# Block-sparse attention with a Swish MLP: all engines in written order, weight casts placed by step, and a V gather shared by two queues

## The chip, the cores and the metric

The kernel runs on one core of a Trainium2 chip. The metric is the device time of one execution in microseconds (us), the median of the runs shown. A core has five engines, each with an instruction queue of its own that it works through in order: TensorE (PE in the profile; its weight loads are PEld), VectorE (DVE), ScalarE (ACT), GpSimd (POOL) and SyncE (SP), which only issues DMAs here. ScalarE and GpSimd issue DMAs too. An instruction waits at the head of its queue until the semaphores it needs are set, and what stands behind it waits as well.

## The reference

Attention over 4 batches, 8 heads, 768 positions and head size 64, in blocks of 32 (24 blocks). A query block sees its neighbours, the first and the last block and three drawn blocks; the first and the last query block see everything. The result, as 3072 rows of 512, goes through a two-layer MLP.

```python
mask = np.abs(blk_i - blk_j) <= 1
mask = mask | (blk_i == 0) | (blk_j == 0) | (blk_i == n_blocks - 1) | (blk_j == n_blocks - 1)
for qb in range(n_blocks):
    for kb in sampled_blocks[qb]:
        mask[qb*32:(qb+1)*32, kb*32:(kb+1)*32] = True
attn = softmax(np.where(mask, scale * q @ k.T, -1e9))
x = (attn @ v)                      # to (3072, 512), heads side by side
h = x @ w_in                        # 512 to 2048
out = (h / (1 + exp(-beta * h))) @ w_out   # 2048 to 512
```

## The kernel before

**Tiling.** A chunk is 128 query rows (4 blocks) of one batch; there are 6 chunks in a batch, taken in the order 1, 2, 0, 5, 3, 4. I call them A, B, C, D, E and F in that order. A step is one chunk with one half of the heads (`Q`, 4 heads). There are 48 steps, 12 for each batch, in this order: A0 B0 A1 B1 C0 D0 C1 D1 E0 E1 F0 F1 (steps 0 to 11), and the same for the next batch (12 to 23, and so on). Chunk C holds the first query block and D the last, so three of their four blocks need gathered data.

**A step** (loop at L635). `scores` writes for each query block the products with its window of three blocks and with five gathered blocks (`KG`: first, last and the three drawn) into two PSUM tiles `sc`; VectorE takes the negative row maximum (`nm`, L334), ScalarE the exponential (`probs`, L337). There are two `sc` buffers, so the next step's scores wait for this step's exponentials. Then `do_A` runs the attention product of three steps earlier (`attend`, L397: `VA` holds the window's V rows and the first block, `VB` the three drawn blocks and the last; then `rec`, L415, and `x`, L416), and `do_T` transposes the previous step's probabilities (`probs_T`; `probsT`, L349). In steps 2 to 5 of each batch `do_G` adds the scores of the first and last query block with all keys (`scg`, `gnm` at L369 and L371, `gp` at L375), also through the `sc` buffers; `do_GT` transposes these one step later.

**MLP.** Finished chunks are transposed (`x_transpose`) and pushed in groups of 2 to 4 as units: `h_unit` (4 products into `hps`, tanh on ScalarE at L457, `g` on VectorE at L459) and `o_unit` (L470, result copied by ScalarE at L476 and written out). `run_moe` spreads them over the steps; the first run in step 7.

**Gathers.** After the second half of a chunk, `prefetch` and `prefetch_v` fetch for the chunk two places on: at the end of step 2 for C, of 3 for D, of 6 for E, of 7 for F, of 9 for the next batch's A, of 11 for its B. `gather_chunk` copies K blocks on GpSimd (L255, L261; `KG` has three buffers). `gather_v` reads rows of `vtab`, a table of V in DRAM that each batch writes (L239). SP issues the DMAs: two or three for `VA`, then one for the last block's rows and one for each drawn block (12 for a chunk, 9 for C and D; the addresses come from registers that SP loads from `sb_eff`). Only chunk A takes `VB` from GpSimd's queue, as four indirect DMAs (L280) whose row lists lie in `idx_b`. `VA` and `VB` have three buffers, so a gather must wait for the attention product of three chunks before: the one for D, issued at the end of step 3, waits for A1's product in step 5, the one for F (end of step 7) for C1's in step 9.

**Weights and next batch.** `load_w_in` and `load_w_out` load 2 MB halves of the float32 weights into a tile of tag `g` and cast them on VectorE (L181, L188); the tag has two buffers, shared with the first loads of v, k and q and later with the MLP's `g`. The first w_in half is issued by SP ahead of the first V gathers, the second by GpSimd in step 0, the w_out halves by GpSimd in steps 2 and 4. `prep_items` prepares the next batch in steps counted from `o`: loads at `o`, v cast and `vtab` written at `o + 2`, k and q cast on GpSimd and transposed on TensorE from `o + 3` to `o + 7`; `o` is 3 for batch 1, 0 for the later ones.

**Row lists.** L111 to L156 are small VectorE operations that turn the drawn block numbers into `sb_eff` and `idx_b`: a drawn block that is visible anyway is replaced by a block of zeros.

**What sets the order.** TensorE, GpSimd and SyncE run in the order in which the program is written; VectorE's and ScalarE's instructions are ordered by the compiler's scheduler:

```python
ctx.enter_context(tc.manual_schedule(engines={ET.PE, ET.Pool, ET.SP}))
```

Of the kernel before, what the change touches and what calls it, by code (L numbers as in the profile page):

```python
# [14 lines left out]
ALU = mybir.AluOpType  # L15
AX = mybir.AxisListType
ET = mybir.EngineType
# [3 lines left out]
def kernel(  # L21
# [11 lines left out]
    nc = tc.nc  # L33

    B, H, S, D = q.shape
    BLK = 32
    NB = S // BLK
# [3 lines left out]
    D_MODEL = H * D  # L41
# [34 lines left out]
    sb_i32 = persist.tile([P, NB * 3, 2], I32, name="sb_i32")  # L76
    nc.sync.dma_start(out=sb_i32.rearrange("p n w -> p (n w)"), in_=sb_all)

    ctx.enter_context(tc.manual_schedule(engines={ET.PE, ET.Pool, ET.SP}))
    identity = persist.tile([P, P], FP16, name="identity")  # L80
    make_identity(nc, identity)

# [10 lines left out]
    def big(name):  # L93
        return g_pool.tile([P, 4096], FP32, tag="g", name=name)
# [60 lines left out]
    idx_b = persist.tile([P, NB], I32, name="idx_b")  # L155
    nc.vector.tensor_copy(out=idx_b, in_=idx_f)  # L156

    def load_regs(t, engine, top, c):
        i0, i1 = max(4 * c, 1), min(4 * c + 4, NB - 1)
# [14 lines left out]
    w_out_r = moe_w_out.rearrange("(c p) m -> p c m", p=P)  # L174
    HF = D_FF // 2

    def load_w_in(hf, eng):
        wst = big("w_in_st").rearrange("p (c f) -> p c f", c=N_DMC)
        eng.dma_start(out=wst, in_=w_in_r[:, :, hf * HF:(hf + 1) * HF])
        for f0 in range(0, HF, 256):  # L180
            nc.vector.tensor_copy(out=w_in_sb[:, :, hf * HF + f0:hf * HF + f0 + 256],  # L181
                                  in_=wst[:, :, f0:f0 + 256])

    def load_w_out(hf):
        wst = big("w_out_st").rearrange("p (c m) -> p c m", m=D_MODEL)
        nc.gpsimd.dma_start(out=wst, in_=w_out_r[:, 8 * hf:8 * hf + 8, :])
        for c0 in range(0, 8, 2):
            nc.vector.tensor_scalar(out=w_out_sb[:, 8 * hf + c0:8 * hf + c0 + 2, :],  # L188
                                    in0=wst[:, c0:c0 + 2, :], scalar1=0.5, scalar2=None,
                                    op0=ALU.mult)  # L190


    zero_sb = persist.tile([BLK, VROW], FP16, name="zero_sb")
# [7 lines left out]
    def prep_tensor(name, b, Q, startup):  # L201
        st = st_tiles.pop((name, b, Q))
        h16 = half_pool.tile([P, 6, 4, D], FP16, tag="h16", name=f"{name}16")
        for h in range(4):
            dst = h16[:, :, h, :]
            src = st[:, h, :, :]
            if startup and name == "k":
                nc.scalar.copy(out=dst, in_=src)
            elif startup:
                nc.vector.tensor_copy(out=dst, in_=src)  # L210
            else:
                nc.gpsimd.tensor_copy(out=dst, in_=src)  # L212
        return h16
# [49 lines left out]
                    in_=kv[:, p0:p1, bass.ds(k_regs[(4 * c + j, r)] * BLK, BLK)])  # L263
        return last

    def gather_v(b, c, indirect=False):
        VA = vg_pool.tile([P, 4, VROW], FP16, tag="VA", name="VA")
        VB = vg_pool.tile([P, 4, VROW], FP16, tag="VB", name="VB")
        js = [j for j in range(4) if 0 < 4 * c + j < NB - 1]
        tab = vtab[b]  # L270

        def rows(row0, nrow, jstep, nj):
            base = tab[row0:row0 + nrow, :]
            ap = list(base.ap)
            return dataclasses.replace(base, ap=[ap[0], [jstep * VROW, nj], ap[1]])

        nj = len(js)
        if indirect:
            for j in js:
                nc.gpsimd.indirect_dma_start(  # L280
                    VB[:, j, :], None, tab[:, :],
                    bass.IndirectOffsetOnAxis(idx_b[:, 4 * c + j:4 * c + j + 1], 0))
# [7 lines left out]
        if indirect:  # L290
            return VA, VB
        v_regs = load_regs(sb_eff, ET.SP, NB, c)
        gb = [j for j in js if 4 * c + j != NB - 2]
        nc.sync.dma_start(out=VB[96:128, gb[0]:gb[0] + len(gb), :],
                          in_=rows(S - BLK, BLK, 0, len(gb)))
        if len(gb) != nj:
            nc.sync.dma_start(out=VB[96:128, NB - 2 - 4 * c, :], in_=tab[S:S + BLK, :])
        for j in js:
            for r in range(3):
                nc.sync.dma_start(  # L300
                    out=VB[BLK * r:BLK * (r + 1), j, :],
                    in_=tab[bass.ds(v_regs[(4 * c + j, r)] * BLK, BLK), :])
        return VA, VB


# [208 lines left out]
    def prep_items(b):  # L514
        def load(n, Q):
            return lambda: load_quad(n, {"q": q, "k": k, "v": v}[n], b, Q, None, nc.gpsimd)
        hold = {}

        def cast(n, Q):
            def f():  # L520
                hold[(n, Q)] = prep_tensor(n, b, Q, False)
            return f

        def tr(n, Q, pr):
            return lambda: transpose_pair(n, b, Q, pr, hold[(n, Q)])
# [12 lines left out]
        return items  # L538
# [12 lines left out]
        prep_v(0, 1, True)  # L551
        write_vtab(0, nc.sync)

    def start_kq1():
        for n in ("k", "q"):
            h16 = prep_tensor(n, 0, 1, True)
            for pr in range(2):
                transpose_pair(n, 0, 1, pr, h16)

    chunk_seq = order  # L560

# [6 lines left out]
    def prefetch_v(n):  # L568
        if n < len(chunk_seq):
            b, c = chunk_seq[n]  # L570
            Vs[(b, c)] = gather_v(b, c, c == 1)

    def start_kg(part):
        for n in range(2):
# [5 lines left out]

    start_kg(0)
    start_v()
    load_w_in(0, nc.sync)
    prefetch_v(0)
    prefetch_v(1)

# [48 lines left out]
    for n, (b, c, Q) in enumerate(steps):  # L635
# [27 lines left out]
        run_moe(units // 2 - units // 4)  # L663
# [53 lines left out]
```

## Time and profile before

| | |
|---|---|
| median of 3 runs | 399.39 us (394.26, 399.39, 401.61) |
| profiled execution | 399.42 us |
| its span, first to last instruction | 397.6 us |
| mean granted TensorE clock | 0.966 |
| HBM traffic over the span | 152 GB/s |
| instructions | 12930 |

Busy time and count by stretch:

| us | TensorE busy | VectorE busy | GpSimd busy | DMA share | GB/s |
|---|---|---|---|---|---|
| 0 to 20 | 6.10 | 9.77 | 11.99 | 0.75 | 247 |
| 20 to 37.4 | 5.98 | 9.89 | 11.62 | 0.94 | 277 |
| 37.4 to 57.4 | 7.96 | 12.37 | 12.48 | 0.98 | 330 |
| 57.4 to 83 | 16.55 | 18.47 | 21.93 | 0.88 | 305 |
| 83 to 106 | 16.37 | 13.92 | 16.09 | 0.57 | 143 |

How to read the lines of the profile that follow: a busy share is the union of an engine's instructions; "in 40 slices" gives one digit for each fortieth of the span (9.94 us), the busy share in tenths. The chain that ended last is followed back from the last instruction, at each step to what released it. In the view of waits a line names the engine and the tile that waited, what released it, the sum in us, how often, and the longest. In a timeline a line has start and duration in us, engine, source line, operation, output and inputs, a count, and in brackets the idle time before it and what ended it.

### The profile page before, as it was taken

Reading aid. Unit: us, or ns where it says so; the run is one execution under the profiler, and the core shown is the slowest. Engines: PE = TensorE matmul, PEld = TensorE weight load, DVE = VectorE, ACT = ScalarE, POOL = GpSimd, SP = SyncE. Lnnn points to the kernel's source line nnn. Section 1 sums busy time; section 2 is a strip of 40 time slices with the busy share of each in tenths; the row PEclk is TensorE's granted clock in tenths of the full one; section 3 lists DMA queues with packets and bytes.
Section 4 is the critical chain, followed back from the end, with each engine's and each line's share of the span. In section 5 each row is a group of like instructions: output and inputs, shape, how many; then the busy total and the mean of one; then the engine's idle time right before and its main releaser. Section 6 shows DMA issues by size and latency. Waiting matters only on the chain.

```text
span 397.6 us, 12930 instructions
## 1 busy us (share of the span) xinstructions
PE 310.0 (78%) x5056; PEld 181.8 (46%) x5056; DVE 239.3 (60%) x499; ACT 202.0 (51%) x401; POOL 170.6 (43%) x472
## 2 busy tenths in 40 slices
PE   1433525685757778978988789999799999999996
PEld 0221313574544435444544455555454555445652
DVE  0938746864777664564777565667677767544330
ACT  3461313375645655542656666546555656444441
POOL 4748939957785194037780193082420400000000
PEclk9999999999978988996999999999899999999999
DMA  7798999756897233057983152454313424100112
GB/s 214 284 335 175 368 357 388 242 110 162 269 333 200 53 88 77 8 144 225 330 292 83 44 136 44 116 156 116 104 26 91 128 57 123 41 28 30 51 54 79
DMA packets 41085, 61.24 MB, mean 154 GB/s; under 512 B 7968, under 2 KB 31648, under 8 KB 41024
## 3 DMA queue, kind: packets, MB, share of 16 engines
q1 hardware_dynamic: 29136, 29.01, 27.9%
q0 software_dynamic: 6368, 25.11, 18.1%
q10 hardware_dynamic: 5520, 6.30, 4.6%
q8 instruction: 40, 0.66, 0.8%
q14 instruction: 21, 0.17, 0.1%
HBM read 50.77 MB, written 9.62 MB: 152 GB/s over the span
## 4 chain that ended last, share of the span: by engine, by line
PE 50%; DVE 23%; ACT 10%; DMA 8%; issue 3%; POOL 3%; another core or an unknown queue 1%; POOLq 0%; SPq 0%; ACTq 0%; DVEq 0%
PE ops L470 17%; PE hps L453 17%; DVE nm L334 6%; DMA w_out_st<-in_moe_w_out_dram 4%; DVE g L459 4%; PE sc L329 3%; PE tp_p L345 3%; ACT gp L375 3%; ACT t_sb L457 3%; ACT probs L337 3%; PE av L397 3%; DVE probsT L349 2%; DMA st_q<-in_q_dram 2%; PE av L409 2%; DVE gnm L369 2%
## 5 line engine op out<-in xcount | busy, mean ns | idle before, releaser
L337 ACT ACTIVATE probs<-sc,nm 128x256 f16<-128x256 f32 x192 | 75.5, 475 | 84.1 <-DVE nm L334 83.1
L459 DVE SCALAR_TENSOR_TENSOR g<-t_sb,hps 128x512 f16<-128x512 f16 (+1 forms) x112 | 67.9, 610 | 66.0 <-ACT t_sb L457 64.6
L453 PE MATMUL hps<-xT,w_in_sb 128*128 128x512 f16 (+1 forms) x448 | 101.3, 363 | 0.8 <-DVE g L459 0.7
L457 ACT ACTIVATE t_sb<-hps,beta_h_sb 128x512 f16<-128x512 f32 (+1 forms) x112 | 69.6, 630 | 49.1 <-PE hps L453 47.3
L470 PE MATMUL ops<-w_out_sb,g 128*128 128x512 f16 x384 | 91.9, 385 | 0.0
L334 DVE TENSOR_REDUCE nm<-sc 128x2 f32<-128x512 f32 x96 | 61.8, 684 | 28.1 <-PE sc L329 28.0
L261 POOL COPY KG<-kT 128x128 f16 (+1 forms) x288 | 72.5, 310 | 0.0
L453 PEld LDWEIGHTS <-w_in_sb 128*128 128x128 f16 x448 | 42.8, 102 | 36.0 <-issue 7.5
L470 PEld LDWEIGHTS <-g 128*128 128x128 f16 x384 | 37.5, 99 | 42.8 <-issue 3.4
L255 POOL COPY KG<-kT 128x512 f16<-128x512 f16 (+2 forms) x52 | 27.6, 562 | 48.8 <-PE sc L329 38.2
L329 PE MATMUL sc<-kT,qT 64*32 64x96 f16 (+1 forms) x832 | 24.4, 223 | 21.4 <-ACT gp L375 17.5
L329 PEld LDWEIGHTS <-qT 64*32 64x32 f16 x1536 | 17.0, 96 | 47.7 <-issue 29.3
L349 DVE COPY probsT<-tp_p 128x1024 f16<-128x1024 f16 x48 | 32.2, 671 | 7.5 <-remote 2.5
L280 POOL DMA_INDIRECT VB<-vtab,idx_b x16 | 15.6, 975 | 43.2 <-PE av L397 33.3
L345 PE MATMUL tp_p<-identity,probs 128*128 128x128 f16 x384 | 33.9, 239 | 0.0
L212 POOL CAST q<-st_q 128x384 f16<-128x384 f32 x24 | 11.2, 511 | 36.3 <-PE tp_k L219 18.5
L329 PE MATMUL sc<-KG,qT 64*32 64x160 f16 x704 | 22.2, 250 | 5.9 <-POOL KG L261 5.0
L476 ACT COPY osb<-ops 128x512 f32<-128x512 f32 x24 | 14.1, 588 | 24.3 <-PE ops L470 24.3
L345 PEld LDWEIGHTS <-probs 128*128 128x128 f16 x384 | 24.8, 107 | 3.2 <-issue 0.4
L375 ACT ACTIVATE gp<-scg,gnm 128x384 f16<-128x384 f32 x32 | 16.8, 577 | 17.9 <-DVE gnm L371 17.9
L397 PE MATMUL av<-VB,probsT 128*32 128x65 f16 x704 | 25.1, 203 | 0.1
L397 PE MATMUL av<-VA,probsT 128*32 128x65 f16 x704 | 23.2, 205 | 1.1 <-issue 1.1
(69 smaller groups left out, 306.6 us busy)
## 6 DMA issues: line engine op xcount, KB each, us to landing
VB<-vtab SPq DMA_DIRECT2D x220, 32.5 KB
VA<-vtab SPq DMA_DIRECT2D x16, 390.0 KB
out_dram<-osb ACTq DMA_DIRECT2D x24, 256.0 KB
st_v<-in_v_dram POOLq DMA_DIRECT2D x6, 768.0 KB
st_k<-in_k_dram POOLq DMA_DIRECT2D x6, 768.0 KB
st_q<-in_q_dram POOLq DMA_DIRECT2D x6, 768.0 KB
w_out_st<-in_moe_w_out_dram POOLq DMA_DIRECT2D x2, 2048.0 KB
VA<-vtab SPq DMA_DIRECT2D x8, 292.5 KB
```

The source lines that it names most:

```text
L261: last = nc.gpsimd.tensor_copy(out=KG[:, j, p0:p1, BLK * (1 + r):BLK * (2 + r)], in_=kv[:, p0:p1, bass.ds(k_regs[(4 * c + j, r)] * BLK, BLK)])
L329: nc.tensor.matmul(o, lhsT=lhsT, rhs=rhs, start=True, stop=True, tile_position=(64 * hp, BLK * j))
L334: nc.vector.tensor_reduce(out=nm[:, hp, :], in_=scs[hp], axis=AX.X, op=ALU.max, negate=True)
L337: nc.scalar.activation(out=pt[:, 2 * pr + hp, :], in_=scs[hp][:, pr, :], func=AF.Exp, bias=nm[:, hp, pr:pr + 1], scale=1.0)
L345: nc.tensor.transpose(out=tp[:, u * 256 + half * P:u * 256 + (half + 1) * P], in_=pt[:, u, half * P:(half + 1) * P], identity=identity)
L349: nc.vector.tensor_copy(out=ptT.rearrange("p u h q -> p (u h q)"), in_=tp)
L375: nc.scalar.activation(out=pv[:, :, 64 * s:64 * (s + 1)], in_=halves[s].rearrange("p (s e) -> p e s", e=6), func=AF.Exp, bias=nm[:, 2:3], ...
L397: nc.tensor.matmul(av[BLK * j:BLK * (j + 1), u, :], lhsT=ptT[:, u, half, BLK * j:BLK * (j + 1)], rhs=V[:, j, h * VW:(h + 1) * VW], start=( ...
L453: nc.tensor.matmul(hp[:, 0:n], lhsT=w_in_sb[:, cc, f * P:(f + 1) * P], rhs=xT_tiles[gi][:, cc, 0:n], start=(cc == 0), stop=(cc == N_DMC - 1))
L457: nc.scalar.activation(out=t_sb[:, 0:n], in_=hp[:, 0:n], func=AF.Tanh, bias=0.0, scale=beta_h_sb[:, f:f + 1])
L459: nc.vector.scalar_tensor_tensor(out=g_tiles[gi][:, f, 0:n], in0=t_sb[:, 0:n], scalar=1.0, in1=hp[:, 0:n], op0=ALU.add, op1=ALU.mult)
L470: nc.tensor.matmul(op, lhsT=g_tiles[gi][:, f, s * P:(s + 1) * P], rhs=w_out_sb[:, f, :], start=(f == 0), stop=(f == N_FFC - 1))
```

## The change

1. VectorE and ScalarE are put into the written order as well, so all five engines follow the program. The row lists (L111 to L156) thereby come first on VectorE.
2. The weight halves are loaded and cast in separate functions. Loads: first w_in half on SP as before, second w_in half on ScalarE's queue in step 0, w_out halves on SP in steps 1 and 4. Casts: steps 1, 3, 5 and 7.
3. The cast of the second half of batch 0's k and q is moved from step 0 to before the loop, its transposes stay in step 0.
4. Every chunk's `VB` is shared: SP reads the rows of its blocks 0 and 1 (one DMA for the last block's rows and three for the drawn blocks, each), GpSimd the blocks 2 and 3 by one indirect DMA each. Before, chunk A was all on GpSimd and the others all on SP. In a batch this makes 11 indirect DMAs in place of 4.
5. The preparation of batch 1 begins in step 4 in place of 3.

```diff
-    ctx.enter_context(tc.manual_schedule(engines={ET.PE, ET.Pool, ET.SP}))
+    ctx.enter_context(tc.manual_schedule(engines={ET.PE, ET.Pool, ET.SP, ET.DVE, ET.Activation}))
...
+    def load_w(kind, hf, eng):
+        if kind == "in":
+            st = big("w_in_st").rearrange("p (c f) -> p c f", c=N_DMC)
+            eng.dma_start(out=st, in_=w_in_r[:, :, hf * HF:(hf + 1) * HF])
+        else:
+            st = big("w_out_st").rearrange("p (c m) -> p c m", m=D_MODEL)
+            eng.dma_start(out=st, in_=w_out_r[:, 8 * hf:8 * hf + 8, :])
+        w_st[(kind, hf)] = st
+
+    def cast_w(kind, hf):
+        st = w_st.pop((kind, hf))
+        if kind == "in":
+            for f0 in range(0, HF, 256):
+                nc.vector.tensor_copy(out=w_in_sb[:, :, hf * HF + f0:hf * HF + f0 + 256],
+                                      in_=st[:, :, f0:f0 + 256])
+        else:
+            for c0 in range(0, 8, 2):
+                nc.vector.tensor_scalar(out=w_out_sb[:, 8 * hf + c0:8 * hf + c0 + 2, :],
+                                        in0=st[:, c0:c0 + 2, :], scalar1=0.5, scalar2=None,
+                                        op0=ALU.mult)
...
-    def gather_v(b, c, indirect=False):
+    def gather_v(b, c):
...
-        if indirect:
-            for j in js:
-                nc.gpsimd.indirect_dma_start(
-                    VB[:, j, :], None, tab[:, :],
-                    bass.IndirectOffsetOnAxis(idx_b[:, 4 * c + j:4 * c + j + 1], 0))
...
+        v_regs = load_regs(sb_eff, ET.SP, NB, c, 2)
         for j in js:
-            for r in range(3):
-                nc.sync.dma_start(
-                    out=VB[BLK * r:BLK * (r + 1), j, :],
-                    in_=tab[bass.ds(v_regs[(4 * c + j, r)] * BLK, BLK), :])
+            if j < 2:
+                g = 4 * c + j
+                nc.sync.dma_start(out=VB[96:128, j, :], in_=tab[S - BLK:S, :])
+                for r in range(3):
+                    nc.sync.dma_start(
+                        out=VB[BLK * r:BLK * (r + 1), j, :],
+                        in_=tab[bass.ds(v_regs[(g, r)] * BLK, BLK), :])
+            else:
+                nc.gpsimd.indirect_dma_start(
+                    VB[:, j, :], None, tab[:, :],
+                    bass.IndirectOffsetOnAxis(idx_b[:, 4 * c + j:4 * c + j + 1], 0))
...
-        o = 3 if b == 1 else 0
+        o = 4 if b == 1 else 0
...
     start_kg(0)
     start_v()
-    load_w_in(0, nc.sync)
+    start_kq1_cast()
+    load_w("in", 0, nc.sync)
     prefetch_v(0)
     prefetch_v(1)
...
         if n == 0:
-            start_kq1()
+            start_kq1_T()
             start_kg(1)
-            load_w_in(1, nc.gpsimd)
-        if n == 2:
-            load_w_out(0)
+            load_w("in", 1, nc.scalar)
+        if n == 1:
+            cast_w("in", 0)
+            load_w("out", 0, nc.sync)
+        if n == 3:
+            cast_w("in", 1)
         if n == 4:
-            load_w_out(1)
+            load_w("out", 1, nc.sync)
+        if n == 5:
+            cast_w("out", 0)
+        if n == 7:
+            cast_w("out", 1)
```

More of the change, by code (lines that the diff above doesn't have):

```diff
@@ L156, with load_regs @@
     nc.vector.tensor_copy(out=idx_b, in_=idx_f)
-    def load_regs(t, engine, top, c):
-        i0, i1 = max(4 * c, 1), min(4 * c + 4, NB - 1)
+    def load_regs(t, engine, top, c, nj=4):
+        i0, i1 = max(4 * c, 1), min(4 * c + nj, NB - 1)
         _, vs = nc.values_load_multi_w_load_instructions(
@@ L175 @@
     HF = D_FF // 2
[L177 to L190, printed above, removed]
+    w_st = {}
+    def load_w(kind, hf, eng):
[17 more added lines that the diff above has]
+                                        op0=ALU.mult)
     zero_sb = persist.tile([BLK, VROW], FP16, name="zero_sb")
@@ L289, in gather_v @@
             nc.sync.dma_start(out=VA[96:128, 1, :], in_=tab[S:S + BLK, :])
[L290 to L297, printed above, removed]
-        for j in js:
-            for r in range(3):
-                nc.sync.dma_start(
-                    out=VB[BLK * r:BLK * (r + 1), j, :],
-                    in_=tab[bass.ds(v_regs[(4 * c + j, r)] * BLK, BLK), :])
+        v_regs = load_regs(sb_eff, ET.SP, NB, c, 2)
+        for j in js:
+            if j < 2:
[9 more added lines that the diff above has]
+                    bass.IndirectOffsetOnAxis(idx_b[:, 4 * c + j:4 * c + j + 1], 0))
         return VA, VB
@@ L552, in start_v, with start_kq1_cast, start_kq1_T @@
         write_vtab(0, nc.sync)
-    def start_kq1():
+    kq1 = {}
+    def start_kq1_cast():
         for n in ("k", "q"):
-            h16 = prep_tensor(n, 0, 1, True)
+            kq1[n] = prep_tensor(n, 0, 1, True)
+    def start_kq1_T():
+        for n in ("k", "q"):
             for pr in range(2):
-                transpose_pair(n, 0, 1, pr, h16)
+                transpose_pair(n, 0, 1, pr, kq1[n])
     chunk_seq = order
@@ L570, in prefetch_v @@
             b, c = chunk_seq[n]
-            Vs[(b, c)] = gather_v(b, c, c == 1)
+            Vs[(b, c)] = gather_v(b, c)
     def start_kg(part):
```

## The prediction

> **What bounds the kernel now.** I read in this order: the page's busy shares and forty slices, the chain that ended last, who waited for whom, who waited for the gathered V, and VectorE's timeline up to 60 us.
>
> ```profile
> PE 310.0 (78%) x5056; PEld 181.8 (46%) x5056; DVE 239.3 (60%) x499; ACT 202.0 (51%) x401; POOL 170.6 (43%) x472
> ...
> PE   1433525685757778978988789999799999999996
> ...
> DMA  7798999756897233057983152454313424100112
> ...
> PE 50%; DVE 23%; ACT 10%; DMA 8%; issue 3%; POOL 3%; another core or an unknown queue 1%; POOLq 0%; SPq 0%; ACTq 0%; DVEq 0%
> ```
>
> TensorE works 310 us of 397.6. Of the 88 us it stands, 37 lie in the first 57 (20 us of work done there), where the 16 DMA engines are nine tenths busy. From 106 us on it is some nine tenths busy, and half of the chain is its own work.
>
> ```profile
> POOL VB L280 <- PE av L397: 33.3, 3, 16.6
> ...
> PE sc L329 <- ACT gp L375: 17.5, 24, 2.0
> ```
> ```profile
> who waited for it (us, times):
>   POOL VB L280: 33.3, 3
>   PEld L397: 0.2, 1
> ```
>
> The attention product waited for a gathered VB 0.2 us in the whole run, so a shorter gather on SP wins nothing by itself. The gather on GpSimd waited three times, 33.3 us in all, for the product that frees its buffer, and everything behind it on GpSimd waited too.
>
> ```profile
> 31.13 6.32 DVE L181 CAST w_in_sb<-w_in_st 128x1024 f16<-128x1024 f32 x4 [4.70 <-DMA w_in_st<-in_moe_w_in_dram]
> 37.37 1.27 DVE L334 TENSOR_REDUCE nm<-sc 128x2 f32<-128x512 f32 x2
> ...
> 47.14 2.77 DVE L181 CAST w_in_sb<-w_in_st 128x1024 f16<-128x1024 f32 x4
> 55.00 2.50 DVE L188 TENSOR_SCALAR w_out_sb<-w_out_st 128x1024 f16<-128x1024 f32 x4 [5.09 <-DMA w_out_st<-in_moe_w_out_dram]
> 57.41 1.28 DVE L334 TENSOR_REDUCE nm<-sc 128x2 f32<-128x512 f32 x2
> ```
>
> I date each step by its first row maximum (L334). Steps 2 to 12 begin at 37.4, 43.0, 57.4, 63.3, 69.6, 76.1, 82.8, 88.1, 93.1, 102.2 and 105.6. A step with global scores takes 5.9 (4 to 5). Step 3 to 4 takes 14.4: VectorE stands in its queue before the first half of w_out while step 4's scores are ready. That is what the change can win.
>
> **Part by part.** The profiled execution took 399.42 us (span 397.6), the median is 399.39; sums are against the former.
>
> Row lists. 24 small VectorE operations (L123 to L156, 0.26 each) ran among the casts from 10.7 to 18.9; now they come first, 5.2 + 6.2 = 11.4, mostly in the wait for q (landed 10.2). Four q casts (1.4) end at 12.8 against 13.0, eight v casts (0.38 each) at 15.9 against 19.5. The vtab write took 4.4 from issue to landing; it now stands on SP behind loads that land until about 18.5 (k1 landed at 16.4, loads come 2.1 apart): landing between 20.4 and 22.9, I take 21.7 against 24.0. The q1 casts (1.15) now precede step 0's maximum and wait for q1: 0.3 later, covered by the longer wait before step 2.
>
> GpSimd at the start. Four indirect gathers as before (two for each of two chunks in place of four for one), so the second half of KG runs 2.3 earlier, 27.4 to 34.5. Three weight loads (1.05, 0.96, 0.89) leave its queue, for SP and ScalarE, where such an issue took 0.37; on ScalarE it precedes step 1's exponential, also under the wait before step 2.
>
> First w_in half, cast in step 1. Issued at 16.4, with the 11.1 of before it lands at 27.6; the second half, on ScalarE's queue from 25, shares the DMA engines, which at half speed makes it 30.2. The casts then meet the KG copies: one cast took 4.26 there against 0.68 alone, copies 0.74 against 0.23. With the 6.3 of before they end at 33.9 to 36.5: step 2 at 35.7, as the KG copies last until 34.5 (gain 1.7), step 3 at 41.4.
>
> Second w_in half, cast in step 3. From 22 on, both halves and two chunks' V (6.3 MB) take 18 us at 350 GB/s, as in the page's fullest slices: landed by 40, no wait. But its 2.8, which ran after the global maxima, now stand before them, on the chain of maximum, exponential and next scores: 5.9 + 2.8 = 8.7 in place of 14.4. Step 4 at 50.1 (gain 7.3), step 5 at 56.0.
>
> First w_out half, issued on SP in step 1 behind 20 gather DMAs (about 38), landed by 55 even with the 17.2 of before, cast in step 5 at 59: no wait, but 2.5 on the chain. Step 6 at 56.0 + 6.3 + 2.5 = 64.8. Step 6 loses its own 3.1 of casts: step 7 at 64.8 + 6.5 - 3.1 = 68.2 (gain 7.9).
>
> Second w_out half, issued on SP in step 4, but behind D's V gather (step 3), which waits for step 5's attention product: 56.5. D's DMAs take 0.9 + 0.8 + 0.7 and six row reads of 0.5 to 1.26 each: issue at 62 to 66.6. From 56.5 on, D's rows (0.9 MB), batch 1's first three loads (2.3) and this half (2.1) take 15 us at 360 GB/s. So it lands (L) between 71 and, at 17.2 from a late issue, 83.8; I take 74, since the other loads are then mostly done. VectorE stands before this cast from 68.2 + 2.6 = 70.8, and behind it queue step 8's maximum and every g: step 8 at L + 2.6 = 76.6 (before 82.8). KG of E is no later: batch 1's loads are issued at 57.9, v lands 4.9 later (as at 102.0 to 106.9), v casts and vtab take 6.4, KG 4.1: 73.7.
>
> Batch 1 prepared a step later, and GpSimd held by V gathers. 16 indirect gathers become 44; 0.97 + 0.30 each, so 28 x 1.27 = 36 us more on an engine that is 43% busy. Most lie beside TensorE's work. One does not: F's gather (end of step 7) waits for C's product in step 9, and the k1 cast of step 8 is queued behind it. After that product GpSimd needs 0.3 + 2.3 + 1.9 + 0.2 = 4.7, then TensorE 1.0 for the transposes, which ended 2.2 after the product in a step without such a wait (83.4 to 85.6): 3.5 lost. One pair of transposes (1.7) moves from step 7 to behind step 8. Step 8 to 12: 22.8 + 1.7 + 3.5 = 28.0. Step 12 at L + 30.6 = 104.6, gain 1.0.
>
> In the two later preparations D's one gather does the same in step 5: product ends 135.6, gather 1.0, cast 1.9, 0.5 between: transposes at 139.0 against 138.0, 2 x 1.0 = 2.0 lost. The k0 cast, some 8 us later than before, ends just before its transposes (129.3); I take nothing, and 1 each for the range.
>
> Written order on VectorE and ScalarE. In eight later steps (15, 17, 26 to 29, 40, 41) the global exponential ran behind one or two tanh (0.69 each) that are written after it; in step 15 it began at 125.74, in written order it could at 125.1: 8 x 0.6 = 4.8 at most. Against that, x (0.41) now precedes probsT, whose copy ends 0.33 later; nine transposes waited for it, 3 at most. Between -4.8 and +3; I take -2.
>
> The sum: -1.0 + 2.0 - 2 = -1.0, so 398.4, told as 398.
>
> The Trainium skill ("SBUF — State Buffer", section "SBUF: two separate sides") speaks against the change: while VectorE runs a two-port copy or cast, GpSimd cannot write the descriptors of its DMAs; the page has 620 ns become 3100. Here sixteen indirect gathers took 945 to 1024 ns each, none shown beside a weight cast, while the KG copies do show the lock. By the page, E's two gathers beside the last cast would cost GpSimd 5 us more, an estimate, and the sum would be up to 403.
>
> **Rivals.** Faster: w_out lands before its turn (L up to 70.8). Step 8 is then bound by KG of E, 73.7 + 0.8 = 74.5; the wait in step 9 hides, and so do the 2.5 us for which VectorE waited at 94.9 on a source that the profile can't name: 74.5 + 22.8 + 1.7 - 2.5 = 96.5, 9.1 gained; with -4.8 for the order and +2.0 it is 387.5. For it: the DMA share was 2 to 3 tenths right after 80 us, so there is room. Against it: the place in SP's queue.
>
> Slower: the second w_out half, behind D's gather on SP, blocks VectorE in step 7. The end moves by L - 75: nothing is gained from 75 on, and from 83 it is over 2% slower. At 66.6 + 17.2 = 83.8 step 12 is at 114.4, and with the order worth nothing the end is 399.4 + 8.8 + 2.0 = 410. For it: SP took 11.3 us for nine row reads at this place. Against it: that bus also carried the loads that now go earlier.
>
> Nothing: the casts merely change places and the waits with them: 399 to 401.
>
> **How the numbers follow.** Forecast 0.43 (own range 391 to 405: L from 71 to 78, the order's bounds, the unnamed 2.5), nothing 0.04, faster 0.29, slower 0.24. 2% is 8 us; the three runs (394.26 to 401.61) let no less be told from no change. Hence faster 0.29, same 0.47, slower 0.24; 386 to 411 takes in both rivals' prices.
>
> **What would show it.** Right: step 4 near 50, no wait for w_out there; a wait for w_out in step 7, its casts ending near 77; TensorE waiting for GpSimd's k cast in step 9; step 12 near 104; indirect gathers still about 1 us. Wrong: step 4 past 55, step 12 under 99 or over 109, or steps 12 to 47 (229.5 us, 105.6 to 335.1) changed by over 5.

## The result, and the profile after

The changed kernel takes 412.5 us (median of 4 runs, 410.56 to 415.19); before, run beside it, takes 398.61 (394.26 to 401.61). The ratio is 1.039, with a 95% interval of 1.028 to 1.050: slower. Here and below a ratio compares fast runs only (now and then a run of any of these kernels takes over 1.5% longer than its fastest), so it differs a little from the quotient of the two medians. The profiled execution took 410.56 us, its span is 408.8 (before 399.42 and 397.6), so the 11.1 us between the two executions lie in the span.

The page of after; first the busy shares, then the slices of TensorE, of its granted clock and of the DMA engines, then the chain that ended last, by engine:

```profile
PE 314.5 (77%) x5056; PEld 183.9 (45%) x5056; DVE 241.6 (59%) x499; ACT 200.2 (49%) x401; POOL 193.4 (47%) x497
...
PE   1442556457757777888997869999799899999996
...
PEclk9999999556897986999999887999989999999999
DMA  7996689935299334035995223265402415000112
...
PE 49%; DVE 22%; DMA 10%; ACT 10%; issue 4%; POOL 2%; SPq 2%; ACTq 0%; another core or an unknown queue 0%; DVEq 0%; POOLq 0%
```

The same work is done on TensorE, VectorE and ScalarE; GpSimd has 23 us more. A slice is 10.2 us. In the sixth, from 51 us, TensorE is busy 5 tenths where before had 2: the early gain. In the eighth and ninth, from 72 to 92 us, it is 4 and 5 where before had 6 and 8, and the granted clock falls to 5 tenths with it.

First maxima of the steps, as in the prediction, in us:

| step | before | forecast | after |
|---|---|---|---|
| 2 | 37.4 | 35.7 | 34.8 |
| 3 | 43.0 | 41.4 | 40.3 |
| 4 | 57.4 | 50.1 | 49.0 |
| 5 | 63.3 | 56.0 | 54.9 |
| 6 | 69.6 | 64.8 | 63.7 |
| 7 | 76.1 | 68.2 | 67.2 |
| 8 | 82.8 | 76.6 | 84.1 |
| 12 | 105.6 | 104.6 | 111.4 |
| 47 | 335.1 | 334.1 | 346.2 |

At step 7 the change is 8.9 us ahead, at step 8 it is 1.3 behind, at step 12 5.8 behind, at step 47 11.1 behind. So there are two places to explain: step 7, and something spread over steps 12 to 47 (234.8 us against 229.5).

VectorE's timeline around step 7 of after (start, duration, the instruction, the idle time ahead of it and what ended that):

```profile
80.16 2.99 DVE L196 TENSOR_SCALAR w_out_sb<-w_out_st 128x1024 f16<-128x1024 f32 x4 [10.52 <-DMA w_out_st<-in_moe_w_out_dram]
83.07 1.07 DVE L462 SCALAR_TENSOR_TENSOR g<-t_sb,hps 128x256 f16<-128x256 f16 x3
84.06 1.28 DVE L337 TENSOR_REDUCE nm<-sc 128x2 f32<-128x512 f32 x2
```

VectorE stands 10.52 us before the second half of w_out, with three g and step 8's maximum queued behind. That half was issued on SP at 62.17, as forecast (62 to 66.6), and VectorE had it at 80.16 instead of 74.

Who waited for whom in after (us in total, times, longest):

```profile
POOL VB L303 <- PE av L400: 111.9, 15, 18.4
...
ACT gp L378 <- DVE gnm L374: 37.3, 16, 4.6
...
PE sc L332 <- ACT gp L378: 22.8, 28, 4.1
```

The global exponential (gp) waited 37.3 us for its maximum, against 17.9 in 15 waits before; the next scores waited 22.8 us for it (17.5 before). GpSimd's indirect gathers waited fifteen times, 111.9 us in all, for the product that frees VB.

### The profile page after: what moved, and what is told of

It reads as the page before. It is cut to its first block, busy times and chain, and to the rows that moved or that the text cites. A ratio compares the mean times of both kernels' runs of the same rounds, so it can differ in the third digit from the quotient of the medians.

```text
span 408.8 us, 12788 instructions
## 1 busy us (share of the span) xinstructions
PE 314.5 (77%) x5056; PEld 183.9 (45%) x5056; DVE 241.6 (59%) x499; ACT 200.2 (49%) x401; POOL 193.4 (47%) x497
## 3 DMA queue, kind: packets, MB, share of 16 engines
q0 software_dynamic: 6128, 22.55, 17.5%
## 4 chain that ended last, share of the span: by engine, by line
PE 49%; DVE 22%; DMA 10%; ACT 10%; issue 4%; POOL 2%; SPq 2%; ACTq 0%; another core or an unknown queue 0%; DVEq 0%; POOLq 0%
PE hps L456 17%; PE ops L473 16%; DVE nm L337 5%; DVE g L462 5%; ACT t_sb L460 4%; DMA VB<-vtab 4%; PE tp_p L348 3%; DVE gnm L372 3%; ACT gp L378 3%; DMA w_in_st<-in_moe_w_in_dram 3%; PE sc L332 3%; PE av L400 3%; DMA st_kq<-in_q_dram 3%; DVE probsT L352 3%; PE av L412 2%
## 5 line engine op out<-in xcount | busy, mean ns | idle before, releaser
L340 ACT ACTIVATE probs<-sc,nm 128x256 f16<-128x256 f32 x192 | 75.2, 474 | 84.7 <-DVE nm L337 82.8
L456 PE MATMUL hps<-xT,w_in_sb 128*128 128x512 f16 (+1 forms) x448 | 104.1, 370 | 1.0 <-DVE g L462 0.7
L303 POOL DMA_INDIRECT VB<-vtab,idx_b x44 | 42.5, 966 | 122.6 <-PE av L400 111.9
L460 ACT ACTIVATE t_sb<-hps,beta_h_sb 128x512 f16<-128x512 f32 (+1 forms) x112 | 68.5, 629 | 40.7 <-PE hps L456 39.7
L269 POOL COPY KG<-kT 128x128 f16 (+1 forms) x288 | 71.4, 294 | 0.0
L473 PEld LDWEIGHTS <-g 128*128 128x128 f16 x384 | 37.4, 99 | 42.1 <-issue 2.3
L332 PE MATMUL sc<-kT,qT 64*32 64x96 f16 (+1 forms) x832 | 24.3, 227 | 27.1 <-ACT gp L378 22.8
L378 ACT ACTIVATE gp<-scg,gnm 128x384 f16<-128x384 f32 x32 | 16.8, 576 | 37.3 <-DVE gnm L374 37.3
L227 PE MATMUL tp_k<-identity,k 128*128 128x128 f16 x96 | 10.9, 276 | 27.5 <-DVE probsT L352 14.9
L400 PE MATMUL av<-VB,probsT 128*32 128x65 f16 x704 | 22.7, 204 | 1.5 <-issue 1.0
```

Of the source, the lines that this page charges most:

```text
L269: last = nc.gpsimd.tensor_copy(out=KG[:, j, p0:p1, BLK * (1 + r):BLK * (2 + r)], in_=kv[:, p0:p1, bass.ds(k_regs[(4 * c + j, r)] * BLK, BLK)])
L303: nc.gpsimd.indirect_dma_start(VB[:, j, :], None, tab[:, :], bass.IndirectOffsetOnAxis(idx_b[:, 4 * c + j:4 * c + j + 1], 0))
L332: nc.tensor.matmul(o, lhsT=lhsT, rhs=rhs, start=True, stop=True, tile_position=(64 * hp, BLK * j))
L340: nc.scalar.activation(out=pt[:, 2 * pr + hp, :], in_=scs[hp][:, pr, :], func=AF.Exp, bias=nm[:, hp, pr:pr + 1], scale=1.0)
L400: nc.tensor.matmul(av[BLK * j:BLK * (j + 1), u, :], lhsT=ptT[:, u, half, BLK * j:BLK * (j + 1)], rhs=V[:, j, h * VW:(h + 1) * VW], start=( ...
L456: nc.tensor.matmul(hp[:, 0:n], lhsT=w_in_sb[:, cc, f * P:(f + 1) * P], rhs=xT_tiles[gi][:, cc, 0:n], start=(cc == 0), stop=(cc == N_DMC - 1))
```

## The experiments

Eighteen runs were made in five sets; within a set all kernels, and the kernel before beside them, ran on one chip. Before took 398.0, 386.4, 390.8, 397.6 and 389.9 us in the five sets in their order, and each ratio is to before of the same set. The kernels with the shared gather do not move with before by the same amount: the changed kernel took 412.5 us beside 398.6, and 407.85 beside 390.8 (f1). So neither times nor ratios of different sets can be compared without care.

**Set 1: the place of w_out on SP, and the gather.**

e1, the second w_out load ahead of D's gather on SP:

```
         if n == 3:
             cast_w("in", 1)
-        if n == 4:
             load_w("out", 1, nc.sync)
```

> The changed kernel with one move: the load of the second w_out half is issued on SP at the end of step 3's cast, ahead of D's V gather, instead of in step 4 behind it. Theory Q (place in SP's queue): it is issued at about 50 and lands by 68, VectorE no longer waits for it in step 7 (10.5 us in the changed kernel), step 8 starts near 75 (KG of chunk E) in place of 84.1, step 12 near 102 in place of 111.4; steps 12 to 47 stay near 235 us; time about 403. Theory G (GpSimd held by the gathers of V is what costs): step 8 is earlier, but TensorE waits the longer for the k cast in step 9, step 12 stays past 107, time about 409. Theory O (written order on VectorE and ScalarE costs): as Q up to step 12, and steps 12 to 47 stay at 235.

408.45 us, 1.027 [1.019, 1.036]. VectorE's timeline of e1:

```profile
69.45 4.12 DVE L196 TENSOR_SCALAR w_out_sb<-w_out_st 128x1024 f16<-128x1024 f32 x4
...
77.74 1.29 DVE L337 TENSOR_REDUCE nm<-sc 128x2 f32<-128x512 f32 x2 [3.17 <-PE sc L332]
```

The wait is gone, and step 8 comes at 77.7, 6.3 earlier; it is now TensorE's scores that are late, for the KG of E that GpSimd finishes at 76.3. But steps 12 to 47 still take 238.4 us (234.8 in after), and the time falls by only 4.1 us: the wait is not the whole loss.

e2, the V gather of before in the changed kernel; e3, e1 and e2 together; e4, e3 with batch 1 prepared a step earlier (`o = 3`):

```
-            Vs[(b, c)] = gather_v(b, c)
+            Vs[(b, c)] = gather_v(b, c, c == 1)
...
-        o = 4 if b == 1 else 0
+        o = 3 if b == 1 else 0
```

> The changed kernel with the V gather of the kernel before (chunk A all on GpSimd, the others all on SP). Q: D's gather has nine reads in place of six, the second w_out half is issued a little later still and lands at 80 to 83, VectorE waits over 10 us, step 8 at 84 to 87; time not under 405. G: no wait of TensorE for a k cast in step 9, steps 8 to 12 take 24 in place of 27.3, steps 12 to 47 return from 234.8 to 229.5; time about 404. O: steps 12 to 47 stay at 235, time about 410.

> Both moves together: second w_out half ahead of D's gather, and the V gather of before. Q and G together: no wait for w_out in step 7, no k cast behind a gather, step 8 at 70 to 75, step 12 at 97 to 100, steps 12 to 47 in 229.5: about 392, faster than the kernel before by 1.5%. O: steps 12 to 47 stay near 235, about 398. Q alone: as the run with the one move, 403.

> As the run with both moves, and batch 1 prepared from step 3 again in place of 4. If the later preparation costs (one pair of transposes behind step 8): steps 8 to 12 are 1.7 shorter, about 390. If the earlier loads of batch 1 share the DMA engines with the second w_out half instead: it lands after 69, VectorE waits in step 7 by 2 to 8 us, and the time is 394 to 400.

419.76 (1.057 [1.049, 1.065]), 413.37 (1.039 [1.030, 1.048]) and 413.08 us (1.039 [1.031, 1.047]). Undoing the shared gather makes e1 4.9 us slower. The old gather puts twelve row reads a chunk on SP, where the change has put the weight loads too: the second w_out half is issued at 68.6 in e3 (54.0 in e1), and step 8 starts 4.7 us later. But step 9 gives most of that back (5.2 us against 9.5), and at step 10 1.1 us is left of it. What is lost beyond lies in steps 10, 22 to 23 and 34, which take 8.6, 14.5 and 8.6 us in e3 and 5.6, 11.0 and 5.8 in e1. Before has long steps at the same places in its first profile (9.1, 16.1 and 7.9), but not in every set, as f4 shows below, so the 4.9 us may hold for a set like this one only. The place of the preparation is worth nothing here. Steps 12 to 47 stay at 237 to 241 us in all of them, so neither edit mends that part.

**Set 2: the order on ScalarE, and the gather alone.**

In after ScalarE is in written order. Its timeline in step 15, first of before, then of after:

```profile
122.47 0.69 ACT L457 ACTIVATE t_sb<-hps,beta_h_sb 128x512 f16<-128x512 f32 x1 [1.24 <-PE hps L453]
...
124.74 0.69 ACT L457 ACTIVATE t_sb<-hps,beta_h_sb 128x512 f16<-128x512 f32 x1 [0.18 <-PE hps L453]
125.74 1.05 ACT L375 ACTIVATE gp<-scg,gnm 128x384 f16<-128x384 f32 x2 [0.31 <-DVE gnm L371]
```
```profile
127.83 0.69 ACT L460 ACTIVATE t_sb<-hps,beta_h_sb 128x512 f16<-128x512 f32 x1 [1.62 <-PE hps L456]
130.56 1.05 ACT L378 ACTIVATE gp<-scg,gnm 128x384 f16<-128x384 f32 x2 [2.05 <-DVE gnm L374]
131.50 1.27 ACT L460 ACTIVATE t_sb<-hps,beta_h_sb 128x512 f16<-128x512 f32 x2
```

Before, three tanh (t_sb) ran while the global maximum was still being taken, and the exponential waited 0.31 us. After, ScalarE stands 2.05 us at the exponential, and both tanh come behind it, and with them their g on VectorE (132.22 to 133.5) and the next step's maximum (133.66). Step 15 takes 9.7 us; it took 8.4.

e5 (on e1), the exponential, and the minimum on VectorE that it needs, written behind the step's remaining MLP units; e6 (on e1), ScalarE given back to the scheduler:

```
             run_moe(units - units // 2 - (units - units // 2) // 2)
+            pend_G.append((g[0], g[1], global_exp(*g[2])))
```
```
-engines={ET.PE, ET.Pool, ET.SP, ET.DVE, ET.Activation}
+engines={ET.PE, ET.Pool, ET.SP, ET.DVE}
```

> Base: the run with the second w_out load ahead of D's gather (408.45 us; its steps 12 to 47 took 238.4 us, before's 229.5). One further edit: in the 16 steps with a global unit the last two operations of global_scores (the tensor_tensor of gnm on VectorE and the two global exponentials on ScalarE) are written after the MoE units of that step instead of ahead of them. Theory O (ScalarE's and VectorE's written order is what costs from step 12 on, since a tanh that is ready stands behind an exponential that waits for gnm): steps 12 to 47 fall to 229 to 233 us, idle time of ScalarE ahead of the global exponential falls from 37 us to below 20, and the time to 400 to 404. Theory C (the lost time is the lower granted clock that the late start leaves behind, 0.92 against 0.97, and the order only shifts idle time between engines): steps 12 to 47 stay at 237 to 240 and the time at 406 to 410.

> Same base (408.45 us). One further edit: ScalarE alone is given back to the scheduler; VectorE, TensorE, GpSimd and SP stay in written order. By the scheduler's own placing the tanh's of a global unit's step stand ahead of its exponential, on ScalarE only. Theory O, if it is ScalarE's order: steps 12 to 47 at 229 to 234 us and the time 400 to 405. If it is VectorE's order that costs: no change, 407 to 410. Theory C: no change, 406 to 410.

e5 took 413.47 us (1.065 [1.059, 1.071]), e6 400.48 (1.035 [1.030, 1.040]), on the same base in the same set. e5 misses what both theories expected: written last, the exponential is late, and TensorE's scores wait longer for the buffers it reads. The wait lists, of e5 and then of e6:

```profile
PE sc L332 <- ACT gp L381: 37.3, 32, 4.5
```
```profile
PE sc L332 <- ACT gp L378: 25.4, 28, 4.3
ACT gp L378 <- DVE gnm L374: 24.3, 14, 4.8
```

The exponential has a narrow place: behind the tanh's that are ready, ahead of those that are not. The scheduler finds it, neither written order does. That is read from the timelines: e6 gives back all of ScalarE's order, not this one place. Steps 12 to 47 take 227.5 us in e6 (241.6 in e5). Their base e1 ran in set 1 only, and by the ratios (1.027 and 1.035) e6 is no better than e1; what the order is worth is shown in set 3, with both kernels in one set.

e7, the kernel of before with the shared gather alone; e8, e5 with `o = 3`:

> The kernel of before with one part of the change alone: the V gather shared by SP and GpSimd (row reads for the first two blocks of a chunk, indirect gathers for the others). Theory H (the shared gather helps, as undoing it in the changed kernel cost 7 us and 5 us): 390 to 396 us, with steps 1 to 4 and 22 to 24 shorter than in before. Theory P (as the prediction had it, the indirect gathers stand ahead of GpSimd's casts and cost some): 400 to 404. In between, 397 to 400: the gather matters only where the head's order is the new one.

> The run with the late global exponential plus the preparation of batch 1 a step earlier again (o = 3, as in before). Theory O with the GpSimd reading (the k cast that stands behind F's gather costs step 9 some 3 us at o = 4): 2 to 4 us below the run with the late exponential alone, 397 to 401. If batch 1's transfers then crowd the two w_out halves (step 8 beyond 79 us): same or up to 4 us above it.

e7 took 401.69 us, 1.038 [1.034, 1.042]: alone, in a set in which before is at its fastest, the shared gather costs as much as the whole change in its own set. e8 took 409.22 (1.057 [1.052, 1.063]), 4.3 below e5, so on this base the place of batch 1's preparation does count. The wait list of e7 shows TensorE's transposes waiting for GpSimd:

```profile
PE tp_k L219 <- POOL KG L261: 5.7, 1, 5.7
PE tp_k L219 <- POOL k L212: 3.1, 3, 1.4
PE tp_q L219 <- POOL q L212: 2.7, 2, 2.4
PE tp_q L219 <- POOL KG L261: 0.4, 1, 0.4
```

11.9 us in all; in the first profile of before only 3.2, all for KG and none for a cast.

**Set 3: after itself, its parts undone, and before with a profile.** f2 is e6's edit on the changed kernel; f3 takes the minimum of the two global maxima with one operand:

```
-        nc.vector.tensor_tensor(out=nm[:, 2:3], in0=nm[:, 0:1], in1=nm[:, 1:2],
-                                op=ALU.min)
+        nc.vector.tensor_reduce(out=nm[:, 2:3], in_=nm[:, 0:2], axis=AX.X, op=ALU.min)
```

The reason for f3, step 29 in after, VectorE and then GpSimd:

```profile
237.84 2.70 DVE L374 TENSOR_TENSOR gnm<-gnm 128x1 f32<-128x1 f32 x1
```
```profile
230.29 0.98 POOL L303 DMA_INDIRECT VB<-vtab,idx_b  x1 [8.15 <-PE av L400]
231.26 1.85 POOL L220 CAST k<-st_k 128x384 f16<-128x384 f32 x4
233.06 3.65 POOL L220 CAST q<-st_q 128x384 f16<-128x384 f32 x8
236.67 1.16 POOL L263 COPY KG<-kT 128x512 f16<-128x512 f16 x2
237.78 2.91 POOL L269 COPY KG<-kT 128x128 f16 x12
```

The gather holds GpSimd until 230.29, so k and q casts and then fourteen KG copies come late, onto the minimum of 128 numbers, which takes 2.70 us instead of 0.16 and ends with the last copies.

> The changed kernel as it is, since the chips of the two sets of runs so far differ (before took 398.0 us on one, 386.4 on the other): the reference for the other three runs of this set. If the ratio to before does not hang on the chip, 1.03 to 1.05. Steps 12 to 47 at 233 to 237 us.

> The changed kernel with ScalarE alone given back to the scheduler; VectorE stays in written order, the wait for the second half of w_out stays. Theory O (ScalarE's written order costs in the steps with a global unit): steps 12 to 47 fall by 6 to 11 us, and the time by as much. Theory C (the clock that the wait at step 7 leaves behind is what costs): at most 2 us.

> The changed kernel with the minimum of the two row maxima (128x1) taken by a tensor_reduce over the two neighbouring columns, one operand in place of two, and the same value. Theory L (VectorE's operation with two operands in SBUF is held out while GpSimd copies KG; at step 29 it took 2.70 us and ended as the copies did): no such operation over 0.5 us any more, step 29 shorter by 2 to 2.7 us, 1.5 to 4 us in all. If it isn't the two operands: it still takes 1 to 3 us beside the copies, and the time stays.

> The kernel of before as it is, for a profile of it on the chip of this set. Ratio 0.99 to 1.01. Should this chip be one on which before takes 386 us: its steps tell whether the 12 us lie in the steps that wait for transfers (1, 3, 22 and 23 by the profile of before: 12.8, 14.4, 6.6 and 9.5 us), or in all steps alike (a higher clock).

f1: 407.85 us, 1.047 [1.040, 1.054]. f2: 403.22, 1.032 [1.027, 1.036], so ScalarE's order is worth 4.6 us in the changed kernel itself by the medians (3.5 without f1's slowest run, 411.28), less than the 6 to 11 expected. The two profiles show only 1.5 of it in steps 12 to 47 (231.0 and 229.5); f1's profiled run, 404.43 us, is the fastest of its four. f3: 407.29, 1.042 [1.033, 1.051]: the long minimum is cured (all sixteen now take 0.15 to 0.16 us), but the time doesn't move beyond what is measurable: in f1's profile that operation took at most 0.90 us, so there was little to win.

f4: 389.53 us, 0.996 [0.991, 1.001]. Its profile (span 388.6) shows where before differs between sets: steps 10, 22 to 23 and 34 take 5.0, 9.7 and 5.6 us there, 9.1, 16.1 and 7.9 in the first profile. In the profiles of kernels with the shared gather steps 22 and 23 take 9.6 to 11.1 us in every set. So the "gain" of 5.0 us that the first pair of profiles shows at steps 22 and 23 is not the change's in a set like this one, and ratios to before of different sets differ by these steps. What makes those steps long, mostly gaps of TensorE that the trace ascribes to no wait, was not settled.

**Set 4: only the place of the indirect gathers.** h1 is f2 and h2 is e7, with the indirect gathers of a chunk issued at the end of the next step, behind that step's casts:

```
-            Vs[(b, c)] = gather_v(b, c)
+            VA, VB, late = gather_v(b, c)
+            Vs[(b, c)] = VA, VB
+            if n < 2:
+                late()
+            else:
+                pend_V.append(late)
...
+        while pend_V:
+            pend_V.popleft()()
         if Q == 1:
             ci = chunk_seq.index((b, c))
```

h3 is h1 with e1's and f3's edits; h4 is the kernel of before with f3's.

> The changed kernel with ScalarE given back to the scheduler (403.22 us, ratio 1.0315, as the run before it with that edit alone), and with the indirect gathers of a chunk issued at the end of the next step, behind that step's casts, instead of ahead of them. Theory D (the casts of k and q stand behind indirect gathers that wait for VB; TensorE's transposes of the next preparation and the KG copies come late for that): TensorE no longer waits for k or q casts at steps 9, 16, 28 and 29, steps 12 to 47 fall by 3 to 6 us, ratio 1.015 to 1.025. Theory H (the shared gather costs nothing by its place; the loss of the gather alone is chance of the clock or of the transfers): ratio 1.03 to 1.04.

> The kernel of before with the shared gather, whose indirect gathers are issued at the end of the next step, behind its casts. The shared gather alone gave 1.038 [1.034, 1.042]; its steps 6 (10.5 us; 6.6 in before), 9 (7.1; 5.0) and 29 (12.8; 8.3) carry most of it. Theory D: these three come back to 6 to 7, 5 and 8 to 10 us, ratio 1.00 to 1.015. Theory H: 1.03 to 1.045.

> The changed kernel with all four edits: the second w_out load ahead of D's gather, ScalarE to the scheduler, the indirect gathers behind the next step's casts, the minimum by one operand. If these causes are the whole loss: ratio 0.985 to 1.01 (1.047 less 1.5 for the wait, 1.2 for the order, 1 to 1.5 for the gathers, 0.5 for the minimum). If a cause is missing: above 1.015.

> The kernel of before with one edit: the minimum of the two row maxima by a tensor_reduce over the two columns. In its second profile that operation took 2.85, 1.29 and 0.90 us at steps 16, 17 and 4, and 0.15 to 0.3 us in the other steps. Theory L: none above 0.3 us, and the time 1 to 4 us lower (0.99 to 0.998). If the time held by the lock lies beside other work: 0.998 to 1.003.

h1: 398.89 us, 1.007 [1.003, 1.011]. h2: 397.58, 1.000 [0.994, 1.006], where e7 had 1.038. Most of that distance is before's, which is 11.2 us slower in this set; from e7 to h2 the time falls by 4.1 us and steps 12 to 47 by 9.2 (231.8 to 222.6). Step 29 comes back as expected (12.8 to 8.3), step 6 in part (10.5 to 8.0), step 9 not (7.1 and 7.5). The transposes no longer wait for casts (8.7 us in f2, nothing in h1); all that is left of e7's 11.9 us in h2's wait list is

```profile
PE tp_k L219 <- POOL KG L261: 0.8, 1, 0.8
```

h3: 390.9 us, 0.981 [0.972, 0.990]: it beats before in this set. Before took 389.5 to 390.8 us in sets 3 and 5, where h3 was not run, so a gain there is not shown. h4: 394.34, 0.994 [0.990, 0.998], a gain of half a per cent. VectorE's and GpSimd's timelines of h3 around step 7:

```profile
72.44 2.68 DVE L196 TENSOR_SCALAR w_out_sb<-w_out_st 128x1024 f16<-128x1024 f32 x4
...
76.03 1.27 DVE L339 TENSOR_REDUCE nm<-sc 128x2 f32<-128x512 f32 x2
```
```profile
66.87 2.89 POOL L269 COPY KG<-kT 128x128 f16 x12
69.70 1.86 POOL L220 CAST k<-st_k 128x384 f16<-128x384 f32 x4
...
72.93 1.07 POOL L305 DMA_INDIRECT VB<-vtab,idx_b  x1 [0.30 <-DMA VB<-vtab]
74.31 1.06 POOL L305 DMA_INDIRECT VB<-vtab,idx_b  x1 [0.30 <-issue]
```

KG of E is ready at 69.8 (76.3 in e1), since batch 1's first loads no longer stand behind D's gather on GpSimd (issued at 42.1, in after at 56.8); the w_out casts wait for nothing, step 8 starts at 76.0 and step 12 at 100.3 (before, first profile: 105.6).

**Set 5: each remaining cause by itself.** i1 moves only the gathers in the changed kernel; i2 is h3 with ScalarE in written order again.

> The changed kernel with one edit: the indirect gathers of a chunk issued at the end of the next step, behind its casts. ScalarE stays in written order, w_out stays where it is. Theory D (their place costs some 2 to 2.5%, as between the runs with ScalarE given back, 1.0315 and 1.0071): 1.015 to 1.03 against the 1.039 and 1.047 of the changed kernel; step 29 at 9 to 11 us. If written order hides the gain: 1.035 or more.

> The changed kernel with the second w_out load ahead of D's gather, the indirect gathers behind the next step's casts and the one-operand minimum; ScalarE and VectorE in written order. Theory O (the written order on ScalarE costs 1 to 1.5% by itself): 0.99 to 1.00, steps 12 to 47 some 4 to 6 us above the 227.8 of the run with ScalarE given back (0.981). If ScalarE's order matters only where the casts come late: 0.975 to 0.987.

i1: 406.43 us, 1.042 [1.035, 1.049], a miss: alone in the changed kernel the place of the gathers gives nothing measurable (f1, in a set with nearly the same before, 407.85). i2: 396.53, 1.013 [1.005, 1.021], 5.6 us above h3 though before was 7.7 faster in its set: ScalarE's order costs also where the casts are in time. The ratio is above the 0.99 to 1.00 expected because before is faster here; steps 12 to 47 take 231.6 us, 3.8 above h3, where 4 to 6 were expected. A likely reading of i1, not shown by a run: while VectorE stands at step 7 and ScalarE at its exponentials, hardly anything waits for a cast that comes earlier, so the gathers' place pays only once those are gone.

From after to the best version the steps that were run are f1 407.85, f2 403.22 (ScalarE's order, 4.6), h1 398.89 (gathers, 4.3), h3 390.90 (w_out's place and the minimum, 8.0): 17.0 us. The middle one spans two sets, and the one that it ends in is the slower for before, so 4.3 is more likely too little than too much; no run shows it within one set.

## Why the prediction was wrong

The forecast was 398 and the range 386 to 411; it came to 412.5. The likeliest case failed, and the rival named slower, w_out behind D's gather on SP, is what step 7 shows. At the L that was measured its price is 5.2 us (80.2 - 75), about half of what was lost. Two steps of the sum failed: the second w_out half, which landed 6.2 us late, and the written order, which cost where it was put down as a gain. Both of the prediction's late signs of being wrong came: step 12 past 109, and steps 12 to 47 changed by over 5.

- **Steps 2 to 7**: right, each within 1.1 us. Casts by step win 8.9 us by step 7, as worked out from the 14.4 us of step 3.
- **The second w_out half, "I take 74"**: this term was mis-sized. L was 80.2. The issue was where it was expected (62.2), but the transfer took 18.0 us, about the 17.2 that the prediction kept as its other end; the DMA share is 1.04 from 64 to 80. The rate was as assumed (352 GB/s from 56.5 to 80.2, forecast 360), the bytes were not: some 8.3 MB went through in that time, where the prediction added up 5.3. It left out what batch 1 issues next, a second k load, a q load and the write of `vtab` (0.8 MB each), and E's rows; so the assumption that the other loads were mostly done was wrong. Everything behind L held: step 8 was put at L + 2.6 and came at L + 3.9, step 12 at L + 30.6 = 110.8 and came at 111.4. With L = 80.2 the sum is 404.6. For the faster rival the prediction cites a DMA share of 2 to 3 tenths right after 80 us; that is a misreading, the slices from 79.5 us on have 5, 6, 8 and 9, and 2 and 3 come only from 129 us.
- **KG of E at 73.7, hidden behind L**: it was ready at 73.8 in after, as forecast, and would have been next. With the wait gone (e1) step 8 stands at 77.7 for KG, done at 76.3, since v landed at 65.0 there, not at 62.8 (57.9 + 4.9) as the prediction had it. So the rival named faster (387.5 at L up to 70.8) was out of reach by that edit alone.
- **F's gather ahead of the k cast, 3.5 us in step 9**: right in size. Step 9 took 8.3 and 8.5 us in two profiles of after, 5.0 in before, and with the gather moved 6.3 in h1 and h3 and 5.2 in i2, though 7.5 in h2.
- **The later preparations, 2.0 us**: probably right in cause and too small. Steps 12 to 47 fall by 3.6 us from f2 to h1, and more in the kernel of before (231.8 in e7, 222.6 in h2), but each pair spans two sets, and i1 gains nothing measurable. What was left out is that late casts push the KG copies onto VectorE's minimum, 2.70 us in step 29 of after. Its price there is open: f3 couldn't show it, since f1's longest was 0.90; in the kernel of before the one-operand minimum gave half a per cent (h4).
- **Written order on VectorE and ScalarE, "I take -2"**: this step failed in its sign. It counted that the exponential could start 0.6 us sooner, and against that only the later probsT on VectorE. It put at nothing what stands behind the exponential: one or two tanh, their g and the next maximum. Giving ScalarE back is worth 4.6 us in after by the medians (f1 to f2). VectorE's order was not tried by itself. In place of -2, +4.6 takes 404.6 to 411.2, against 410.56 measured; that closeness is partly chance, since the same pair of profiles holds 7.1 us gained at steps 22, 23 and 34 (16.1 to 11.1 and 7.9 to 5.8), and 5.8 us of losses that neither term covers (steps 12 to 47 grew by 5.3; 5.3 + 7.1 - 4.6 - 2.0), whose cause stays open.
- **"A shorter gather on SP wins nothing by itself"**: e7 and h2 (1.038 and 1.000) bear it out. e3, with the old gather, is 4.9 us slower than e1: its row reads hold up the second w_out half on SP, and most of the loss lies in steps that are long in before only in some sets.
- **The Trainium skill's rule ("SBUF — State Buffer", section "SBUF: two separate sides")**, by which GpSimd's descriptors would wait for VectorE's casts: the runs show little of it. In after no indirect gather ran beside a weight cast, and the 44 took 0.97 us on average, 1.03 at most. In other runs ten of them did and took 1.07 to 1.47, the longest in step 3 of h2, h3's two 1.07 and 1.06. By these, two such gathers would cost some 1 us at most, an estimate, not the 5 of the prediction. The place of the gather in GpSimd's queue cost time, its own length hardly any.

## What to carry to other kernels

When an engine is taken from a scheduler into written order, list for each instruction that may wait what is queued behind it and ready: a saving at the waiting instruction is paid for by all of those. A transfer whose consumer stands in an in-order queue belongs ahead of everything on its own queue that waits for compute, and its duration is best taken from a stretch where the DMA engines are as full as they will be. A gather that waits for a free buffer goes behind the casts of the next step, which somebody needs sooner; undo several causes together before calling one of them harmless. And where the baseline itself takes different times from set to set, as before does here, test a cause by two variants within one set.

## What the runs showed of the hardware

A VectorE operation on 128 x 1 with two operands in SBUF took up to 3.94 us (e7, step 29) while GpSimd copied KG without a break, and ended with the copies; beside GpSimd's casts of k and q it took up to 2.85 (f4, step 16), in most steps 0.15 to 0.5. With one operand it took 0.14 to 0.16 in all four profiles that have it (f3, h3, h4, i2). The Trainium skill has both ("SBUF — State Buffer", section "Who interferes with whom": two SBUF inputs contend with GpSimd's reads, a reduction doesn't), but by the same page (section "SBUF: two separate sides") the engine that came first holds the port for one instruction, and here the wait lasted over twelve copies in after and fourteen in e7, most of about 0.29 us.

The granted clock fell in after, and no single stand of TensorE explains it. The windows of after around step 7 (start and end; time; busy PE, PEld, DVE, ACT, POOL; clock; DMA share; GB/s):

```profile
64.00:80.00 16.00, 10.80 (x224) 8.26 (x213) 5.41 (x12) 4.39 (x11) 14.35 (x33) 0.79 1.04 380
80.00:84.00 4.00, 0.00 (x0) 0.00 (x0) 3.84 (x7) 0.00 (x0) 4.00 (x9) 0.50 1.06 251
84.00:91.00 7.00, 4.47 (x90) 3.20 (x90) 3.79 (x10) 4.50 (x9) 1.18 (x5) 0.55 0.11 35
```

It was at 0.50 with TensorE idle from 80 to 84 us and still at 0.55 over the next 7, where before had 1.00. But it had fallen before that stand: it was 1.00 up to 73 us and 0.50 from 74 to 78, when TensorE was busy 3.4 of the 4 us. Before kept 1.00 through a longer stand (52 to 62 us, 1.0 us busy). In e1, without the stand at step 7, the clock was 0.74 to 0.77 from 57 to 106, 0.76 over the whole of it, which is also what after has there (before 0.97). Nor did a lower mean clock always go with a longer time: the first profile of before has 0.966 and a span of 397.6 us, the second (f4) 0.915 and 388.6. What makes the clock fall, and what share of the lost time is the clock's, stays open.
